# Loading the V projection's weights in two halves of their rows

## The chip, the core and the metric

The kernel runs on one core of a Trainium2 chip. The metric is the device time of one execution in microseconds (us). Each verdict rests on several executions of both kernels on the same chip, and a difference under 2% counts as "same". The profile is of one execution; its span, from first to last instruction, is about 2 us shorter than the device time. The engines are PE (matmuls), DVE (elementwise work and statistics), ACT (activations and copies), POOL, and SP, which here does nothing but issue transfers (DMA).

## The reference, cut to what matters

A transformer block on 2048 tokens of width 512: an adaptive layer norm, attention in which each token looks back at 8 positions two apart, and a gated MLP.

```python
qkv = x @ wqkv                  # wqkv: 512 x 1536, columns of Q, K and V
logits = einsum(q, k at pos - 2*w)          # w = 0..7, 32 heads of 16
o = softmax(logits) @ (v at pos - 2*w);  x = x + ga * (o @ wo)
h = gelu(h2 @ w_gate) * (h2 @ w_up);     x = x + gb * (h @ w_down)
```

## The kernel before

All operations are first collected by a planner, which decides the order on each engine; then they are emitted in that order. The loads from HBM are issued by SP, in this order at the start: rows 0 to 255 of x, the 1 MB of modulation weights (`wm01`), wq in two halves, rows 256 to 511 of x, wk in two halves, wv in one piece, rows 512 to 1023 of x (called **x2** here), and further x and weights.

```python
def load_wqkv(b, p, cuts=1):
    m = DT // cuts
    for i in range(cuts):
        dma(524e3 / cuts, lambda i=i: nc.sync.dma_start(
            out=wqkv[b][:, m * i:m * i + m, :],
            in_=A_wqkv[m * i * P:m * (i + 1) * P, b * D:(b + 1) * D].rearrange("(o p) n -> p o n", p=P)),
            w=[(wqkv[b], k) for k in range(m * i, m * i + m)], pri=p + 0.02 * i)
load_wqkv(0, -998.65, 2)
def load_wk():                       # one operation for the planner, two transfers
    for i in range(2):
        nc.sync.dma_start(out=wqkv[1][:, 2 * i:2 * i + 2, :],
                          in_=A_wqkv[2 * i * P:2 * (i + 1) * P, D:2 * D].rearrange("(o p) n -> p o n", p=P))
dma(524e3, load_wk, w=[(wqkv[1], k) for k in range(DT)], pri=L["wk"])
load_wqkv(2, L["wv"])                # wv, one transfer of 512 KB
load_x(2, 4, L["x1"])
load_x(4, 8, L["x2"])
# ... cut: the other loads ...
# the first 256 tokens: each matmul group is cut by blocks of 128 rows of the weights
cut = ((0,), (1,), (2,), (3,)) if b == 0 else ((0, 1), (2, 3))
for k, dts in enumerate(cut):
    pe(0.23 * len(dts), lambda ...: mm(b, j, ps, range(nj), dts),
       r=[(wqkv[b], dt) for dt in dts] + [(hT[g], dt) for dt in dts], w=[ps], pri=p + 0.01 * k)
```

The tile framework adds the semaphores. It has eight for transfers and hands them out in rotation, in the order of issue; a transfer waits at its issue until the eighth one before it has landed.

## Time and profile before

| | before |
|---|---|
| device time, median of 3 | 242.34 us (242.17 to 242.43) |
| span of the profiled execution | 240.2 us |
| PE busy | 98% of the span |
| PE idle ahead of the first wv matmul | 0.30 us |
| x2 issued by SP, landed | 5.41, 13.66 us |
| PE's steady stretch from | 32.30 us |

The important rows are in the prediction. Four more are from the timelines of the kernel before (start, length, engine, instruction; in brackets the idle time before it and what ended it).

```profile
5.41 2.64 SPq L379 DMA_DIRECT2D x_sg<-in_A_x_dram  x2
...
18.46 0.39 PE L573 MATMUL tp<-ident,xn 128*128 128x128 bf16 x4
...
26.36 0.38 PE L832 MATMUL LT<-Lb,NB 128*128 128x512 bf16 x1 [0.56 <-DVE Lb L827]
...
32.30 1.02 PE L689 MATMUL qkv_ps<-hT,wq 128*128 128x512 bf16 x4 [0.32 <-ACT hT L559]
```

The first row merges SP's issues of the two x loads after wv, of which x2's is the first. The second is four transposes of DVE's `xn`. The third is the first matmul that waits for the maximum of the logits (`Lb`), the end of DVE's long run. The fourth is the last wait of PE before its steady stretch.

### The profile page before, as it was taken

How to read it: one execution, taken by the hardware profiler on the slowest of the kernel's cores; microseconds unless marked ns; L12 is line 12 of the kernel's file. 1: busy time of each engine (PE TensorE's matmuls, PEld its weight loads, DVE VectorE, ACT ScalarE, POOL GpSimd, SP SyncE). 2: the span in 40 equal slices, each digit the busy share in tenths (PEclk: the TensorE clock that was granted, in tenths of full speed). 3: DMA queues.
4: the chain of work that ended last, by engine and by line, in shares of the span. 5: the costliest groups of instructions: out<-in, count | busy, mean ns of one | idle time of the engine just before them, and what ended most of it. 6: DMA issues, size and time to landing. Idle time of an engine off the chain costs nothing.

```text
span 240.2 us, 4193 instructions
## 1 busy us (share of the span) xinstructions
PE 234.3 (98%) x1588; PEld 126.3 (53%) x1588; DVE 160.9 (67%) x307; ACT 159.4 (66%) x298; POOL 12.8 (5%) x35
## 2 busy tenths in 40 slices
PE   7999999999999999999999999999999999999994
PEld 2888545567674557664444444444444444444442
DVE  3699869849997799981899897489455122222222
ACT  4488797699785878669866676846767801666400
POOL 6000210100001000020000002000011000000000
PEclk9999999999999999999999999999999999999999
DMA  6999999999932139512129404100003010000011
GB/s 218 361 367 401 244 305 317 240 257 217 235 60 44 44 87 258 102 36 55 44 60 213 85 3 80 51 22 26 0 1 73 17 44 21 22 0 3 0 44 44
DMA packets 34997, 28.23 MB, mean 118 GB/s; under 512 B 11041, under 2 KB 33314, under 8 KB 34978
## 3 DMA queue, kind: packets, MB, share of 16 engines
q1 hardware_dynamic: 34976, 27.97, 45.8%
q8 instruction: 12, 0.20, 0.4%
q14 instruction: 7, 0.06, 0.1%
q10 hardware_dynamic: 2, 0.00, 0.0%
HBM read 21.40 MB, written 4.21 MB: 107 GB/s over the span
## 4 chain that ended last, share of the span: by engine, by line
PE 86%; DVE 5%; DMA 3%; SPq 2%; ACT 1%; issue 1%; DVEq 0%
PE u_ps L973 20%; PE g_ps L973 20%; PE y_ps L999 20%; PE qkv_ps L689 12%; PE x_ps L932 6%; DMA x_sg<-in_A_x_dram 3%; PE o_ps L907 3%; PE LT L784 3%; DVE st L628 2%; DVE pq L772 1%; ACT hT L559 1%; DVE xn L544 1%; PE ss L867 1%; SPq L423 1%; PE LT L832 1%
## 5 line engine op out<-in xcount | busy, mean ns | idle before, releaser
L973 PE MATMUL g_ps<-h2T,Wg 128*128 128x512 bf16 (+1 forms) x280 | 57.7, 337 | 0.0
L973 PE MATMUL u_ps<-h2T,Wu 128*128 128x512 bf16 (+1 forms) x280 | 57.7, 337 | 0.0
L999 PE MATMUL y_ps<-WdP,hht 128*128 128x512 bf16 (+2 forms) x238 | 50.3, 367 | 0.0
L982 ACT ACTIVATE gl<-g_ps 128x512 bf16<-128x512 f32 x56 | 33.5, 598 | 24.2 <-PE g_ps L973 19.3
L986 DVE TENSOR_TENSOR hht<-gl,ub 128x512 bf16<-128x512 bf16 x56 | 23.4, 422 | 31.0 <-ACT ub L985 30.8
L985 ACT CAST ub<-u_ps 128x512 bf16<-128x512 f32 x56 | 32.8, 585 | 15.3 <-PE u_ps L973 15.1
L973 PEld LDWEIGHTS <-Wg 128*128 128x128 bf16 x280 | 27.1, 98 | 23.3 <-issue 1.7
L973 PEld LDWEIGHTS <-Wu 128*128 128x128 bf16 x280 | 27.1, 98 | 22.2 <-issue 1.3
L772 DVE TENSOR_TENSOR pq<-qT,kT 128x2048 bf16<-128x2048 bf16 x32 | 38.1, 1218 | 0.0
L999 PEld LDWEIGHTS <-hht 128*128 128x128 bf16 x238 | 22.7, 98 | 25.8 <-issue 0.4
L888 DVE TENSOR_TENSOR pv<-e,vR 128x2048 bf16<-128x2048 bf16 x24 | 28.4, 1219 | 0.1
L1007 DVE TENSOR_TENSOR x_sg<-y_ps,x_sg 128x512 bf16<-128x512 f32 (+2 forms) x17 | 10.8, 657 | 26.1 <-PE y_ps L999 26.1
L549 POOL TENSOR_TENSOR rstd<-rstd,neghalf 128x2 f32<-128x2 f32 x12 | 8.8, 731 | 169.2 <-DVE rstd L947 106.7
L689 PE MATMUL qkv_ps<-hT,wq 128*128 128x512 bf16 (+1 forms) x80 | 16.5, 336 | 0.5 <-ACT hT L559 0.5
L689 PE MATMUL qkv_ps<-hT,wk 128*128 128x512 bf16 (+1 forms) x80 | 16.3, 337 | 0.2 <-ACT hT L559 0.2
L689 PE MATMUL qkv_ps<-hT,wv 128*128 128x512 bf16 (+1 forms) x80 | 15.6, 337 | 0.3 <-DMA wv<-in_A_wqkv_dram 0.3
L932 PE MATMUL x_ps<-woP,oT 128*128 128x512 bf16 x64 | 15.3, 379 | 0.0
L939 ACT ACTIVATE xn<-x_sg 128x512 bf16<-128x512 bf16 x16 | 10.0, 627 | 4.2 <-DVE x_sg L936 4.0
L605 ACT ACTIVATE h2T<-h2T,modT,scl 128x512 bf16<-128x512 bf16 (+1 forms) x16 | 11.0, 753 | 2.1 <-DMA h2T<-xn 2.1
L628 DVE BATCH_NORM_STATS2 st<-x_sg 128x6 f32<-128x512 bf16 x16 | 10.2, 681 | 2.8 <-DMA x_sg<-in_A_x_dram 2.8
L689 PEld LDWEIGHTS <-wk 128*128 128x128 bf16 x80 | 8.7, 113 | 5.2 <-issue 0.7
L689 PEld LDWEIGHTS <-wq 128*128 128x128 bf16 x80 | 8.7, 113 | 5.2 <-issue 1.1
(100 smaller groups left out, 217.1 us busy)
## 6 DMA issues: line engine op xcount, KB each, us to landing
vR<-scr SPq DMA_DIRECT2D x24, 260.0 KB, 5.1
vR<-scr SPq DMA_DIRECT2D x8, 264.0 KB, 8.6
out_dram<-x_sg SPq DMA_DIRECT2D x15, 128.0 KB, 1.7
Wu<-in_B_w_up_dram SPq DMA_DIRECT2D x4, 448.0 KB, 8.1
scr<-vT SPq DMA_DIRECT2D x7, 256.0 KB, 7.1
Wg<-in_B_w_gate_dram SPq DMA_DIRECT2D x4, 448.0 KB, 6.5
WdP<-in_B_w_down_dram SPq DMA_DIRECT2D x2, 896.0 KB, 9.8
x_sg<-in_A_x_dram SPq DMA_DIRECT2D x3, 512.0 KB, 8.2
```

Source lines behind the costliest of these rows:

```text
L605: act(act_us(n, 2), lambda dt=dt: nc.scalar.activation(out=dst[:, :, dt, :], in_=dst[:, :, dt, :], func=ACT.Identity, scale=scl[:, off // ...
L628: stats = lambda i=i, st=st, tok=tok: nc.vector.bn_stats(out=st[:, i, :], in_=xrow(tok + P * i))
L689: nc.tensor.matmul(shaped(ps[:, jl, :], g, XB1), lhsT=wqkv[b][:, dt, j + jl:D:4], rhs=columns(hT[g], g, dt, XB1), start=(dt == 0 and (jl = ...
L772: dve(1.145, lambda j=j, wg=wg, no=no, t=pq[m]: nc.vector.tensor_tensor(out=t[:], in0=_ap(q[g][:, j, :], [[0, no], [1, n]]), in1=_ap(kT[:, ...
L888: dve(1.145, lambda jj=jj, jl=jl, wg=wg, t=pv[m]: nc.vector.tensor_tensor(out=t[:], in0=_ap(e[:, wg, :], [[0, 4], [1, n]]), in1=vR[g][jj][ ...
L932: nc.tensor.matmul(x1_ps[:], lhsT=oT[:, j, c4 * P:(c4 + 1) * P], rhs=woP[:, j, :], start=(j == 0), stop=(j == 3))
L973: nc.tensor.matmul(shaped(ps[:, f, :], g, XB2), lhsT=Wt[:, dt, ft * P:(ft + 1) * P], rhs=columns(h2[g], g, dt, XB2), start=(dt == 0), stop ...
L982: act(act_us(SG), lambda gl=gl, ps=gu[0]: nc.scalar.activation(out=gl[:], in_=flat(ps), func=ACT.Gelu_apprx_tanh), r=[gu[0]], w=[gl], pri= ...
L985: act(act_us(SG), lambda ub=ub, ps=gu[1]: nc.scalar.copy(out=ub[:], in_=flat(ps)), r=[gu[1]], w=[ub], pri=p)
L986: dve(0.339, lambda gl=gl, ub=ub, ht=hh[u // 2], u=u: nc.vector.tensor_tensor(out=ht[:, u % 2, :], in0=gl[:], in1=ub[:], op=ALU.mult), r=[ ...
L999: nc.tensor.matmul(y_ps[:], lhsT=hh[u // 2][:, u % 2, f * n + c4 * P:f * n + (c4 + 1) * P], rhs=WdP[:, ft, lo_d:hi_d], start=(ft == 0), st ...
L1007: dve(0.07 + nd * 1.041e-3, lambda y_row=y_row, y_ps=y_ps: nc.vector.tensor_tensor(out=y_row(), in0=y_ps[:], in1=y_row(), op=ALU.add), r=[ ...
```

## The change

Its intent: PE waits for wv at 12 us, so let the first half of wv's rows arrive earlier. The diff, cut to what acts (the rest adds options that are switched off):

```diff
-    load_wqkv(2, L["wv"])
+    def load_wv():
+        for i in range(2):
+            nc.sync.dma_start(out=wqkv[2][:, 2 * i:2 * i + 2, :],
+                              in_=A_wqkv[2 * i * P:2 * (i + 1) * P, 2 * D:].rearrange("(o p) n -> p o n", p=P))
+
+    dma(524e3, load_wv, w=[(wqkv[2], k) for k in range(DT)], pri=L["wv"])
     # ... cut ...
+TREE = ()
+WIDE = 0
```

Instructions and their order are the same on every engine but SP, which has one transfer more.

More of the change, by code (lines that the diff above doesn't have):

```diff
@@ L804, in emit_attention, with most, tree @@
         us = 0.072 + n * 0.52e-3
-        dve(us, lambda: nc.vector.tensor_tensor(out=Lb[:, 0, :], in0=Lb[:, 0, :], in1=Lb[:, 1, :], op=ALU.max),
-            r=[Lb], w=[Lb], pri=p)
+        def most(out, a, b):
+            nc.vector.tensor_tensor(out=out, in0=a, in1=b, op=ALU.max)
+        def tree():
+            most(Lb[:, 0, :], Lb[:, 0, :], Lb[:, 1, :])
+            most(Lb[0:64, 1, :], Lb[0:64, 0, :], Lb[64:128, 0, :])
+            most(Lb[0:32, 0, :], Lb[0:32, 1, :], Lb[32:64, 1, :])
+        joint = g in TREE
+        if joint:
+            dve(3 * us + 0.3, tree, r=[Lb], w=[Lb], pri=p)
+        else:
+            dve(us, lambda: most(Lb[:, 0, :], Lb[:, 0, :], Lb[:, 1, :]), r=[Lb], w=[Lb], pri=p)
         if g in DVEMAX:
@@ L809, in emit_attention @@
             top, all4 = mx
-            def most(out, a, b):
-                nc.vector.tensor_tensor(out=out, in0=a, in1=b, op=ALU.max)
             def spread():
@@ L824, in emit_attention @@
         else:
-            dve(us, lambda: nc.vector.tensor_tensor(out=Lb[0:64, 1, :], in0=Lb[0:64, 0, :], in1=Lb[64:128, 0, :],
-                                                    op=ALU.max), r=[Lb], w=[Lb], pri=p)
-            dve(us, lambda: nc.vector.tensor_tensor(out=Lb[0:32, 0, :], in0=Lb[0:32, 1, :], in1=Lb[32:64, 1, :],
-                                                    op=ALU.max), r=[Lb], w=[Lb], pri=p)
+            if not joint:
+                dve(us, lambda: most(Lb[0:64, 1, :], Lb[0:64, 0, :], Lb[64:128, 0, :]), r=[Lb], w=[Lb], pri=p)
+                dve(us, lambda: most(Lb[0:32, 0, :], Lb[0:32, 1, :], Lb[32:64, 1, :]), r=[Lb], w=[Lb], pri=p)
             def sub_max():
@@ L1018 @@
             mod_keep(mod0, -969)
-            dve(0.34, lambda: nc.vector.tensor_copy(out=wide.t[:, 0, :].rearrange("p (t n) -> p t n", n=P),
+            (gp if WIDE else dve)(0.34, lambda: (nc.gpsimd if WIDE else nc.vector).tensor_copy(out=wide.t[:, 0, :].rearrange("p (t n) -> p t n", n=P),
                                                     in_=_ap(scT[:], [[1, 4], [0, P]])), r=[scT, hT[0]], w=[(wide, 0)],
```

## The prediction

> **What bounds the kernel now.** I read the page first, then the chain of work that ended last in order of time, then the timelines of SP, PE and DVE over the first 30 us, because the change touches only a load that is issued at 4.8 us. From the page (busy time with its share of the span; the shares of the chain by engine; the waits ahead of the group of matmuls that read wv):
>
> ```profile
> span 240.2 us, 4193 instructions
> PE 234.3 (98%) x1588; PEld 126.3 (53%) x1588; DVE 160.9 (67%) x307; ACT 159.4 (66%) x298; POOL 12.8 (5%) x35
> ...
> PE 86%; DVE 5%; DMA 3%; SPq 2%; ACT 1%; issue 1%; DVEq 0%
> ...
> L689 PE MATMUL qkv_ps<-hT,wv 128*128 128x512 bf16 (+1 forms) x80 | 15.6, 337 | 0.3 <-DMA wv<-in_A_wqkv_dram 0.3
> ```
>
> PE is the bound: 86% of the chain, and idle for only 240.2 - 234.3 = 5.9 us of the span. The wait that the change can touch is in the last line: over the whole run PE stood still 0.3 us for wv, once.
>
> Where the other 14% of the chain lies is in the chain in order of time (start, length, what; all us):
>
> ```profile
> 4.83 0.53 SPq L423
> 5.37 0.04 issue
> 5.41 8.25 DMA x_sg<-in_A_x_dram
> 13.66 0.02 issue
> 13.68 2.47 DVE st L628 x4
> ...
> 26.03 0.29 DVE Lb L827
> 26.32 0.04 issue
> 26.36 0.38 PE LT L832
> ...
> 30.23 2.03 ACT hT L559 x3
> 32.26 0.04 issue
> 32.30 7.07 PE qkv_ps L689 x32
> ```
>
> The reader is to see three stretches. SP issues loads one after another; wv (L423) is the last before the 512 KB piece of x, rows 512 to 1023, which I call x2. The landing of x2 at 13.66 starts a run of DVE that lasts to 26.3 us. A short hand-over over PE and ACT follows, and from 32.30 on PE works almost without a gap to the end. So the end moves if x2's landing moves, or the DVE run after it, or the PE work after 32.3. It does not move for PE work done earlier.
>
> Three rows of the timelines (start, length, engine, instruction, and in brackets the idle time before it and what ended it) show the disputed moment:
>
> ```profile
> 12.20 0.63 PE L689 MATMUL qkv_ps<-hT,wv 128*128 128x256 bf16 x4 [0.30 <-DMA wv<-in_A_wqkv_dram]
> ...
> 13.68 2.47 DVE L628 BATCH_NORM_STATS2 st<-x_sg 128x6 f32<-128x512 bf16 x4 [0.27 <-DMA x_sg<-in_A_x_dram]
> ...
> 25.60 0.41 DVE L544 TENSOR_SCALAR xn<-x_sg,mv,rstd 128x512 bf16<-128x512 bf16 x1 [0.51 <-DVE Lb L825]
> ```
>
> PE waits for wv, DVE waits for x2. On DVE's timeline no row between 13.68 and 25.60 has a bracket: in that run DVE never waits for PE or ACT.
>
> **What the Trainium skill says.** (1) "Perfetto Trace Analysis", section DMA Optimizations: splitting DMAs may let some work start sooner, "If DMA engines are generally idle". Here they are not: the page's DMA row is 9 tenths in each slice from 6 to 66 us. A split can bring the first half forward, not the data behind it. (2) "DMA: Bandwidth & Descriptors", section Queues, rings and completion order: each engine consumes descriptors in ring order. The trace agrees: the loads from HBM land in the order of issue, about 0.75 us for each 256 KB (worked out below). (3) The same page, section Why a DMA increments its semaphore by 16 and not by 1: transfers in flight should not share a semaphore. The program has eight of them in rotation, so a transfer waits at issue for the eighth one before it; the trace agrees, with the third x load issued at 6.93, just after the weight load of 1.32 landed at 1.32 + 5.6 = 6.92. (4) "Perfetto Trace Analysis", section DMA Instruction — HWDGE (DVE, Sync): the reported window of such an instruction holds its issue, not the movement of its data. Indeed wv's 512 KB take SP 0.53 us, but PE gets them at 12.20.
>
> **The change part by part.** I compared the order of instructions of both programs. PE, DVE, ACT and POOL have the same instructions in the same order; SP has one more, two loads of wv of 256 KB where there was one of 512 KB. The rest of the diff is switched off (an empty TREE, WIDE = 0). The planner still sees one operation of 524e3 bytes. What moves is this:
>
> (a) First half earlier. Landings before, as issue plus time to landing: the two halves of wk 3.65 + 6.2 = 9.9 and 4.17 + 6.5 = 10.65; x2 5.41 + 8.25 = 13.66. Between wk and x2 lie wv and x2, 1 MB in 3.0 us, so 0.75 us for 256 KB. The whole wv lands at about 10.65 + 1.5 = 12.15, the first half at about 11.4. The new program's first eight wv matmuls need only that half (the wait for the second semaphore stands after them). PE has finished wk at 11.90, so they can start there: the gap of 0.30 us goes. The transposes behind them start at about 12.37 instead of 12.67, because xn is ready at 11.53 + 0.74 = 12.27, and ACT's hT at about 13.0 instead of 13.31. **Gain on PE: 0.30 us; on the path: 0.** DVE is busy or waiting for x2 whatever PE does, and its next result for PE is Lb at 26.03 + 0.29 = 26.32. There PE already waits 0.56 us; it would wait up to 0.86 us instead.
>
> (b) One more transfer in the rotation of eight. Before, x2's issue waited for the transfer eight places ahead, the first piece of x, landed at 0.81 + 3.0 = 3.8, so it did not wait. Now it has the place after, and waits for the 1 MB weight load that lands at 6.92. **x2's issue moves from 5.41 to about 6.95.** In its turn the third x load waits for wq's first half (1.81 + 5.8 = 7.6) and comes at about 7.65 instead of 6.93. The later ones are bounded by landings at 8.4, 9.15, 9.9, 10.65, 11.4 and 12.15, which lie earlier than their old issue times from 10.19 on, so SP has caught up there. Two halves cost SP 0.48 us each (like wq) for one issue of 0.53: 0.4 us, hidden in the same wait.
>
> (c) x2's landing. At 6.95 seven pieces of 256 KB stand ahead of it (wq twice, x, wk twice, wv twice): 7 x 0.75 = 5.2 us, to 12.15. The first load of the program landed 3.0 us after its issue with nothing ahead, of which I estimate 3.0 - 0.75 = 2.25 for everything but the data; x2 could so start to arrive at 9.2. It needs its turn at 12.15 only. **Slack 2.9 us, cost 0.**
>
> (d) Sixteen more tiny completion packets. wk in two pieces and x2 in one run at the same rate, as (a) assumes and the 1.44 us of the next 512 KB (landing at 6.93 + 8.2 = 15.1) bears out: at most 0.05 us on x2's landing.
>
> After wv every transfer waits for the same one as before, as both have moved one place. The sum for the end: 0 (a) + 0 (b, c) + 0 to 0.05 (d).
>
> **Rivals.** *The late issue counts.* If x2 kept its 8.25 us from issue, it would land at 6.95 + 8.25 = 15.2 and the DVE run would begin 1.5 us later: 243.9 us. For it: x2's issue is in the chain. Against it: the 8.25 us are mostly the bytes ahead, by (c), and DMA is 9 tenths busy. Chance about 6%. *The gap on PE counts in full*, if some wait of the stretch to 32 us hangs on PE or ACT after all: 242.34 - 0.3 = 242.0. For it: hT (L559) on ACT is in the chain at 30.23. Against it: that hT comes after Lb and the DVE run. Chance about 15%. *A later shift*: scr<-vT, which SP issues at 16.29 once ACT has written vT, can come 0.3 us earlier and pull the Wu loads behind it. The queue then still holds about 5 us of loads (the 512 KB issued at 10.90 took 9.2 us to land), so nothing lands earlier; worth 0.1 us either way.
>
> **Range and chances.** The sum leaves the time of before: 242.34, and I set 242.3, as the second rival pulls a little lower. The three runs of before span 0.26 us. The second rival gives 0.3 down, (d) and a part of the first rival 0.5 up: 241.8 to 242.9. Two per cent are 4.8 us. A gain of that size would need nearly all of PE's 5.9 us of idle time, a loss three times the first rival: 1% faster, 97.5% same, 1.5% slower.
>
> **What would show it right or wrong.** Right: PE's bracket of 0.30 ahead of wv is gone (a), x2's issue starts at about 6.95 with a time to landing near 6.7 (b), DVE's st still starts at 13.68 within 0.1 (c), PE waits about 0.86 ahead of L832's first matmul, and PE's steady stretch starts at 32.3. Wrong: x2 landing near 15 shows the first rival; Lb ready before 26.2 with x2 landing unchanged shows a dependence of DVE on PE that I do not see; a gap on PE after 40 us would be something that I have not considered.

## The result, and the profile after

The changed kernel took 242.15 us (median of 3; 241.96 to 242.34), before 242.34. The ratio is 0.9993, with a 95% interval of 0.9971 to 1.0016. The change is within the noise.

The page after. (The smaller number of instructions and PE's lower busy time are 18 matmuls missing from the record; the program has as many as before.)

```profile
span 240.0 us, 4177 instructions
...
PE 232.5 (97%) x1570; PEld 125.6 (52%) x1588; DVE 160.9 (67%) x307; ACT 159.1 (66%) x298; POOL 12.8 (5%) x35
...
PE 86%; DVE 5%; DMA 5%; ACT 1%; issue 1%; SPq 0%; DVEq 0%
...
L697 PE MATMUL qkv_ps<-hT,wv 128*128 128x512 bf16 (+1 forms) x79 | 15.5, 337 | 0.1
```

The wait for wv is gone from the last line: no releaser is named any more. In the chain's shares DMA has grown from 3% to 5% and SP's issue has gone from 2% to 0. The chain in order of time shows why:

```profile
1.32 5.33 DMA wm<-in_w_mod_dram
6.65 0.02 issue
6.67 6.77 DMA x_sg<-in_A_x_dram
13.44 0.02 issue
13.46 2.47 DVE st L636 x4
...
26.14 0.38 PE LT L848
...
32.08 2.10 PE qkv_ps L697 x9
```

x2 is issued at 6.67, released by the landing of the modulation weights at 1.32 + 5.33 = 6.65. Before, it was issued at 5.41. Yet it lands at 13.44, so the 1.26 us of later issue are taken off the queue time behind it (6.77 us from issue to landing in place of 8.25). The three PE rows of interest, in the timeline of the changed kernel:

```profile
11.49 0.60 PE L697 MATMUL qkv_ps<-hT,wv 128*128 128x256 bf16 x4
...
17.73 0.59 PE L581 MATMUL tp<-ident,xn 128*128 128x128 bf16 x4
...
26.14 0.38 PE L848 MATMUL LT<-Lb,NB 128*128 128x512 bf16 x1 [0.87 <-DVE Lb L815]
```

wv's first matmul has no bracket, and the wait for `Lb` has grown from 0.56 to 0.87 us. The bracket of 0.30 us was not all that PE had lost to wv, though. From the first wk matmul to the first wv matmul it took 12.20 - 9.99 = 2.21 us before and takes 11.49 - 9.72 = 1.77 us now, 0.44 us less (9.99 and 9.72 are the starts of the wk rows just ahead). Some of it is waited away earlier: the four transposes at 17.73 take 0.59 us in place of 0.39, because inside this merged row they wait 0.20 us for DVE's `xn`. So what PE won at 12 us it waits away at 18 and at 26 us.

This execution runs 0.2 us ahead of the profiled one of before from the start of DVE's run on. That is not the change: the modulation weights, which are issued before anything that changed, landed at 6.65 in place of 6.92. From that landing to x2's landing it is 13.44 - 6.65 = 6.79 us after, and 13.66 - 6.92 = 6.74 before.

### The profile page after: what moved, and what is told of

It reads as the page before. It is cut to its first block, busy times and chain, and to the rows that moved or that the text cites. A ratio compares the mean times of both kernels' runs of the same rounds, so it can differ in the third digit from the quotient of the medians.

```text
span 240.0 us, 4177 instructions
## 1 busy us (share of the span) xinstructions
PE 232.5 (97%) x1570; PEld 125.6 (52%) x1588; DVE 160.9 (67%) x307; ACT 159.1 (66%) x298; POOL 12.8 (5%) x35
## 4 chain that ended last, share of the span: by engine, by line
PE 86%; DVE 5%; DMA 5%; ACT 1%; issue 1%; SPq 0%; DVEq 0%
PE u_ps L989 20%; PE g_ps L989 20%; PE y_ps L1015 20%; PE qkv_ps L697 12%; PE x_ps L948 6%; PE o_ps L923 3%; DMA x_sg<-in_A_x_dram 3%; PE LT L792 3%; DVE st L636 2%; DMA wm<-in_w_mod_dram 2%; DVE pq L780 1%; ACT hT L567 1%; DVE xn L552 1%; PE ss L883 1%; PE LT L848 1%
## 5 line engine op out<-in xcount | busy, mean ns | idle before, releaser
L1015 PE MATMUL y_ps<-WdP,hht 128*128 128x512 bf16 (+2 forms) x230 | 49.8, 366 | 0.4
```

What stands on the lines that cost most here:

```text
L1015: nc.tensor.matmul(y_ps[:], lhsT=hh[u // 2][:, u % 2, f * n + c4 * P:f * n + (c4 + 1) * P], rhs=WdP[:, ft, lo_d:hi_d], start=(ft == 0), st ...
```

## The experiments

The theory: the end hangs on a chain of rigid pieces: x2's landing, then DVE's run and the hand-over to PE's steady stretch, then PE to the end. The change moves x2's issue, not its landing, and moves PE's work where PE has slack. The rivals: the late issue counts; PE's gap counts; something else binds. Eleven kernels were run, all correct.

**The changed kernel again**, with five rounds.

> The changed kernel once more, with more rounds. My theory (the end hangs on when x2 lands, and the split does not move that): a ratio to before of 1.000 within 0.15%, and in the trace x2 landing about 6.8 us after the 1 MB weight load, as in both traces so far (13.66 - 6.92 = 6.74 before, 13.44 - 6.65 = 6.79 after). Rival (the PE gap of 0.30 us counts in full): a ratio of 0.9988 or lower.

Measured: 242.2 us (median of 6) against 242.17, ratio 0.9993 (0.9967 to 1.002). x2 landed 13.54 - 6.75 = 6.79 us after the modulation weights. So no movement is seen, but an interval of 0.5% can't rule out a gain of 0.1% in the times; the traces can, and they show the 0.3 us waited away (0.88 us ahead of `Lb` in this one).

**The extra transfer without the useful half**: wv in halves of its partitions.

```diff
-        for i in range(2):
-            nc.sync.dma_start(out=wqkv[2][:, 2 * i:2 * i + 2, :], in_=<rows 256 i to 256 i + 255>)
+        for lo in (0, 64):
+            nc.sync.dma_start(out=wqkv[2][lo:lo + 64, :, :], in_=<partitions lo to lo + 63>)
```

> wv in two halves of its partitions in place of its rows: the extra transfer in the rotation without a first half that is of use, since every row block needs both. My theory: x2 issued at about 6.7 to 6.9 as in the changed kernel, x2 landing unmoved (6.8 us after the 1 MB weight load), PE's gap of about 0.3 us ahead of wv back, and the gap ahead of L848 0.5 to 0.6 us in place of 0.87; time 242.2 +- 0.3. Rival (the gap counts): 242.5.

Measured: 243.49 us. The expectation failed, because the transfer itself is slower. These are windows of the changed kernel and then of this one (window, length, busy time by engine, granted clock, mean DMA share, GB/s in the last column):

```profile
10.00:11.00 1.00, 1.00 (x12) 1.00 (x10) 0.49 (x3) 0.97 (x4) 0.00 (x0) 1.00 1.10 346
11.00:12.00 1.00, 1.00 (x13) 0.99 (x11) 0.79 (x3) 0.80 (x3) 0.00 (x0) 1.00 1.11 350
```

```profile
10.00:11.00 1.00, 0.97 (x8) 0.71 (x8) 0.69 (x3) 1.00 (x3) 0.00 (x0) 1.00 1.13 213
11.00:12.00 1.00, 0.90 (x8) 0.80 (x8) 0.71 (x2) 0.46 (x3) 0.00 (x0) 1.00 1.13 233
```

While the half-width transfers run, the queue moves 213 to 233 GB/s in place of 346 to 350, at the same DMA share. x2 was issued at 6.87, much as in the changed kernel, and landed 1.0 us late for the bytes ahead of it:

```profile
13.21 0.60 PE L697 MATMUL qkv_ps<-hT,wv 128*128 128x256 bf16 x4 [1.04 <-DMA wv<-in_A_wqkv_dram]
...
14.60 2.47 DVE L636 BATCH_NORM_STATS2 st<-x_sg 128x6 f32<-128x512 bf16 x4 [0.92 <-DMA x_sg<-in_A_x_dram]
...
33.24 1.02 PE L697 MATMUL qkv_ps<-hT,wq 128*128 128x512 bf16 x4 [0.32 <-ACT hT L567]
```

As a test of the rotation it is void. It serves as another: x2 about 1.1 us late gives a steady stretch 1.1 us late.

**More places in the rotation**: wv in four pieces, then in eight (each row block in two halves of its partitions).

```diff
-        for i in range(2): <256 rows each>
+        for dt in range(4): nc.sync.dma_start(out=wqkv[2][:, dt, :], in_=<128 rows>)            # four
+        for k in range(8): nc.sync.dma_start(out=wqkv[2][lo:lo + 64, dt, :], in_=<64 rows>)     # eight
```

> wv in four pieces of one row block: x2 waits for wq's second half and is issued at about 8.2. The queue then still holds data until about 12.0 and a transfer needs some 2.3 us from issue to its first byte. My theory (the queue covers a late issue): x2 lands 6.8 us after the 1 MB weight load as before; time 242.2 +- 0.3. Rival (x2 keeps its 6.8 us from issue to landing): x2 lands at about 15.0, time 243.7.

Measured: 242.08 us. x2 was issued at 8.28, 2.9 us later than in the kernel before, and landed at 13.53, 6.78 us after the modulation weights; the DVE run began at 13.56 and PE's steady stretch at 32.19. This late issue is covered.

> wv in eight pieces (row block by half of the partitions): the eighth piece waits for wk's second half (about 10.5) and x2 waits for the first piece of wv (about 10.8), so x2 is issued at about 11. Now the queue runs dry: first byte of x2 not before about 13.2, landing about 14.7, 1.2 us late. My theory: the DVE run and PE's steady stretch both start 1.0 to 1.5 us late, time 243.2 to 243.7. Rival (x2 keeps 6.8 us from its issue): 17.8, time 246.5. Rival (x2's landing does not set the end): 242.2.

Measured: 244.47 us (median of 4), ratio 1.0098 (1.0059 to 1.0137). The direction is right: x2 is issued at 10.87 and the queue runs dry (95 GB/s from 11 to 12 us, 123 from 12 to 13). But it landed at 16.04, not 14.7. I had not counted that half-width pieces are slow, and there was more, which the next run shows without them.

**Only the rotation**: five loads of 16 rows of 128 bytes ahead of x2.

```diff
     def load_x2():
+        for k in range(5):
+            nc.sync.dma_start(out=spare[0:16, k, :], in_=A_wqkv[0:16, 64 * k:64 * k + 64])
         nc.sync.dma_start(out=xs[1][:], in_=<rows 512 to 1023 of x>)
```

> The changed kernel with five loads of 16 rows of 128 bytes between wv and x2: nearly no bytes, but five more places in the rotation, so x2 waits for wk's second half and is issued at about 10.5, with full-width transfers throughout (the eight pieces and the partition halves also made wv itself slower, which I had not counted). My theory: the queue holds data until about 12.0, x2 needs some 2.3 us plus 1.5 us of data from its issue, so it lands at about 14.2, 0.7 us late, the stretch from DVE's statistics to PE's steady stretch stays 18.6 us, time 242.7 to 243.1. Rival (x2 keeps 6.8 us from its issue): 17.3, time 246. Rival (the late issue is covered here too): 242.2.

Measured: 244.79 us (median of 4), ratio 1.0087 (1.0056 to 1.0118). x2 is issued at 10.61. Windows and rows of its profile:

```profile
11.00:12.00 1.00, 1.00 (x12) 1.00 (x11) 0.73 (x2) 0.78 (x3) 0.00 (x0) 1.00 0.55 84
12.00:13.00 1.00, 1.00 (x16) 0.99 (x14) 0.89 (x1) 0.75 (x3) 0.00 (x0) 1.00 0.79 254
...
20.20:23.60 3.40, 3.31 (x16) 1.84 (x17) 3.40 (x7) 2.24 (x5) 0.00 (x0) 0.50 1.04 358
```

```profile
16.04 1.88 DVE L644 BATCH_NORM_STATS2 st<-x_sg 128x6 f32<-128x512 bf16 x3 [2.70 <-DMA x_sg<-in_A_x_dram]
...
20.29 0.71 PE L589 MATMUL tp<-ident,xn 128*128 128x128 bf16 x4 [2.23 <-DVE xn L560]
...
35.17 1.02 PE L705 MATMUL qkv_ps<-hT,wq 128*128 128x512 bf16 x4 [0.32 <-ACT hT L575]
```

The queue is dry at 11 to 12 us (84 GB/s): here is the edge beyond which a late issue counts, as the theory has it. The size was wrong by two things. The trace records the completion of a transfer in sixteen parts. Of x2's, fifteen came by 14.54, close to the 14.2 expected, and one at 16.02. In the same stretch a 16 KB packet of the instruction queue runs from 11.67 for 1.99 us. That this packet held back the last part is likely. The eleven other traces without an early disturbance have one such packet too, of 1.0 to 1.1 us, later in the run. There the last part of a load is at most 0.4 us behind the other fifteen ahead of the packet, and 0.8 to 1.5 us behind them on the first or second load that lands after it. But the record doesn't name what carried a part, and in the two disturbed traces at the end of this section a part trails by 1.4 to 1.9 us with no such packet before it, so the cause stays inferred. And PE, left idle for 2.23 us, has a granted clock of 0.50 from 20.2 to 23.6 us; the run from DVE's statistics to the steady stretch takes 19.1 us in place of 18.6. The eight pieces show the same: 2.56 us of idle PE ahead of 20.30, then a clock of 0.50 from 19.8 to 23.2.

Both profiles caught the worse of two cases. Of the four executions with five small loads, the one with a granted clock of 0.998 took 243.69 us, the three at 0.991 to 0.993 took 244.69 to 245.12. Of the four of the eight pieces, the two at 0.998 and 0.999 took 243.9 and 244.23 us, the two at 0.993 took 244.72 and 246.14. With 242.17 us for the kernel before on the eight pieces' chip, their late x2 costs 1.7 us or more also where the clock holds; for the five small loads one such execution is too little to say.

The runs together, from the same rows of each profile; the last five are described below. "Run" is steady stretch minus statistics, "rest" is span minus steady stretch:

| kernel | x2 issued | DVE statistics | PE steady from | run | rest |
|---|---|---|---|---|---|
| before | 5.41 | 13.68 | 32.30 | 18.62 | 207.9 |
| changed | 6.67 | 13.46 | 32.08 | 18.62 | 207.9 |
| changed, again | 6.76 | 13.56 | 32.19 | 18.63 | 208.1 |
| four pieces | 8.28 | 13.56 | 32.19 | 18.63 | 207.8 |
| partition halves | 6.87 | 14.60 | 33.24 | 18.64 | 208.2 |
| five small loads | 10.61 | 16.04 | 35.17 | 19.13 | 207.6 |
| eight pieces | 10.87 | 16.06 | 34.97 | 18.91 | 207.7 |
| three fillers on PE | 6.70 | 13.49 | 32.13 | 18.64 | 207.9 |
| twelve fillers on PE | 6.75 | 13.55 | 33.68 | 20.13 | 207.9 |
| x2 ahead of wv | 4.97 | 13.39 | 32.54 | 19.15 | 208.7 |
| wv and x2 woven | 5.37, 7.46 | 13.12 | 31.74 | 18.62 | 208.6 |
| reads of vR earlier | 6.59 | 13.38 | 32.01 | 18.63 | 207.9 |

In the first seven rows the run and the rest are rigid, to within 0.1 us and 0.3 us, as long as the clock holds. There x2's landing is what sets the end, and it doesn't follow its issue until the queue is dry. The run is longer where PE was made late by more than its slack (twelve fillers, x2 ahead of wv), and the rest where PE waits for `pv` (x2 ahead of wv, woven).

**PE's slack**: three and twelve more matmuls of 128x512 ahead of the first wv matmul of the changed kernel.

```diff
             def mm(b, j, ps, jls, dts):
+                if g == 0 and b == 2 and j == 0 and dts == (0, 1):
+                    filler(ps.t, 3)          # 12 in the second kernel
```

> The changed kernel with three more matmuls of 128x512 (0.65 us) on PE just ahead of the first wv matmul: PE is made later than in the kernel before, with all loads as changed. My theory (PE has slack up to Lb): the gap ahead of L850 or so (the matmul that waits for Lb) shrinks from 0.87 to about 0.2 us, PE's steady stretch starts where it did, time 242.2 +- 0.3. Rival (PE's time here counts): 242.8.

Measured: 242.07 us, with the steady stretch from 32.13. The wait for `Lb` shrank to 0.44 us:

```profile
18.40 0.39 PE L581 MATMUL tp<-ident,xn 128*128 128x128 bf16 x4
...
26.19 0.38 PE L850 MATMUL LT<-Lb,NB 128*128 128x512 bf16 x1 [0.44 <-DVE Lb L817]
```

It lost 0.43 us for 0.65 us of matmuls; I had expected it to fall to 0.2. The first wv matmul came the whole 0.65 us later (12.17 in place of 11.49, in an execution 0.03 us behind). The other 0.2 us came out of the wait for `xn`: the four transposes take 0.39 us again.

> The same with twelve matmuls (2.6 us). My theory: the slack of 0.87 us on PE is used up and the rest, 2.6 - 0.9 = 1.7 us, reaches the end: 243.9 (243.5 to 244.3). Rival (the slack is much larger, other engines wait only for DMA): 242.2. Rival (everything counts): 244.8.

Measured: 243.59 us (median of 4), ratio 1.0067 (1.0053 to 1.0081). The steady stretch began at 33.68 with x2 landing unmoved (statistics at 13.55), so 1.5 us of the 2.6 came through and 1.1 us was slack. Here DVE does wait inside its run:

```profile
18.63 1.38 DVE L552 TENSOR_SCALAR xn<-x_sg,mv,rstd 128x512 bf16<-128x512 bf16 x4 [1.22 <-ACT rstd L562]
```

ACT computes this `rstd` after `hT`, for which it waited 2.84 us for PE's transposes; and the matmul ahead of which PE waited for `Lb` has no bracket any more. So PE's lateness reaches the end by way of ACT, not through the wait for `Lb` alone. Both sides of the theory's claim are shown: PE may be later by 0.65 us at no cost, and is not free without bound.

**x2 ahead of wv**, with wv's halves behind it.

```diff
-    wv rows 0-255; wv rows 256-511; x2
+    x2; wv rows 0-255; wv rows 256-511
```

> The changed kernel with x2 issued ahead of wv's halves: x2 lands 1.5 us earlier, wv 1.5 us later. My theory: DVE loses its gap of 0.27 us ahead of its statistics, but PE waits for wv about 1.2 us more, uses up its slack of 0.87 us ahead of the matmul that waits for Lb, and gives back what DVE won: time 242.0 to 242.5. Rival (only DVE counts): 241.9. Rival (PE's wait counts): 243.4.

Measured: 243.25 us, above what I expected and nearer to the last rival. In its timeline of PE:

```profile
13.03 0.63 PE L709 MATMUL qkv_ps<-hT,wv 128*128 128x256 bf16 x4 [1.07 <-DMA wv<-in_A_wqkv_dram]
...
32.54 1.02 PE L709 MATMUL qkv_ps<-hT,wq 128*128 128x512 bf16 x4 [0.31 <-ACT hT L579]
...
40.92 0.40 PE L935 MATMUL o_ps<-pv,F 128*32 128x256 bf16 x8 [0.54 <-DVE pv L922]
```

PE's wait for wv (1.07 us) was larger than its slack allowed, DVE waited 0.26 us for ACT's `rstd` at 17.50, and the steady stretch began 0.4 us late. A wait appeared that shows in neither kernel: 0.54 us for `pv`, DVE's product with the V tiles `vR`, which are written to memory and read back. `vR` itself landed 1.2 us later than in the changed kernel (36.12 in place of 34.95). That second chain is close behind the first.

**wv and x2 woven**, both in halves.

```diff
-    wv rows 0-255; wv rows 256-511; x2
+    wv rows 0-255; x2 rows 512-767; wv rows 256-511; x2 rows 768-1023
```

> The changed kernel with x2 in two halves too, woven with wv's: wv rows 0 to 255, x2 rows 512 to 767, wv rows 256 to 511, x2 rows 768 to 1023. wv's second half lands 0.75 us later than now, x2's first half 0.75 us earlier than x2 now. My theory: DVE's gap of 0.29 us ahead of the statistics goes and PE has no new wait (its second half of wv is needed 0.9 us after the transposes start), so the end comes 0.25 us earlier: 241.9 to 242.0, ratio to before 0.998 to 0.999. Rival (the DVE run hangs on something else): unchanged, ratio 0.9993 to 1.000.

Measured: 242.3 us (median of 5), ratio 1.0012 (0.9999 to 1.0026). The rows of its timelines of DVE and PE:

```profile
13.12 2.46 DVE L648 BATCH_NORM_STATS2 st<-x_sg 128x6 f32<-128x512 bf16 x4
...
31.74 1.02 PE L709 MATMUL qkv_ps<-hT,wq 128*128 128x512 bf16 x4 [0.31 <-ACT hT L579]
...
35.40 4.63 DVE L922 TENSOR_TENSOR pv<-e,vR 128x2048 bf16<-128x2048 bf16 x4 [1.82 <-DMA vR<-scr]
...
40.08 0.40 PE L935 MATMUL o_ps<-pv,F 128*32 128x256 bf16 x8 [0.50 <-DVE pv L922]
```

DVE's gap is gone and the steady stretch begins 0.34 us earlier than in the changed kernel, as expected. Then PE waits 0.50 us for `pv`, and `pv` waits for the reads of `vR`, which land at 35.28, as in the kernel before. The gain is given back there: my theory was right for the first 32 us and wrong for the end. The two chains are in fact nearly level in the kernel before: its merged row of 32 `o_ps` matmuls lasts 1.20 us, against 1.06 where `vR` lands by 34.6, so I take PE to wait about 0.14 us for `pv` there already.

**The reads of vR earlier**: the last quarter of w_up's load issued behind the four reads of `vR`, alone and with the woven order.

```diff
-    Wu rows 0-127; 128-255; 256-383; 384-511; woP; vR x4
+    Wu rows 0-127; 128-255; 256-383; woP; vR x4; Wu rows 384-511
```

> The changed kernel with the last quarter of Wu issued behind the four vR reads in place of ahead of them, a control for the next run: vR is read about 1 us earlier. My theory: in the changed kernel PE's o_ps matmuls do not wait for pv, so an earlier vR is worth nothing: 242.15, ratio to before 0.998 to 1.000.

Measured: 241.9 us (median of 4; 241.75 to 242.03), ratio 0.9976 (0.995 to 1.0001). `vR` landed 0.9 us earlier than in the changed kernel (34.07 in place of 34.95), and DVE's statistics (13.38) and the steady stretch (32.01) are again 18.63 us apart, with a rest of 207.9 us as in the changed kernel, so the trace shows no gain. The interval holds 1, and three of the twelve runs of before on that chip had a granted clock of 0.993 or less, so whether this change alone gains is open.

> The woven order of wv and x2 together with the early vR reads. The woven run started PE's steady stretch at 31.74 in place of 32.1 to 32.2, and then waited 0.50 us at 40.08 for pv, which hangs on the vR reads (landed 35.27). My theory: with vR 1 us earlier this wait goes, and the end comes 0.3 to 0.4 us earlier than in the changed kernel: ratio to before 0.997 to 0.9985, about 241.7. Rival (the gain is lost at another wait after 40 us): ratio 0.999 to 1.001.

Measured: 241.9 us (median of 7), ratio 0.9969 (0.9943 to 0.9995). The profiled execution was disturbed, so the kernel was run once more:

> The woven order with the early vR reads once more, because the profiled execution of the first run was disturbed (its 1 MB weight load landed 1.8 us late[...], and PE's clock was halved for 3.4 us). My theory: in an undisturbed execution PE's steady stretch starts at 31.6 to 31.8 and runs without the wait of 0.50 us at 40 us, the span is 207.9 us longer than that start, 239.5 to 239.7, and the ratio to before is 0.9975 to 0.999. Rival (the wait at 40 us stays or another takes its place): span 240.0 or more, ratio 0.999 to 1.001.

Measured: 241.92 us (median of 7) against 242.53, ratio 0.9971 (0.9946 to 0.9997). The profile again caught a disturbed execution (244.68 us): one of sixteen parts of the first large load landed 1.4 us behind the others, at 8.25, and PE's clock was 0.50 from 10.4 to 13.8. In that trace the steady stretch runs without the wait for `pv`, but this shows nothing: it began at 34.80, 3 us later than in the woven run, with `vR` landed at 35.35. Of the fourteen executions of the two submissions, ten have a granted clock of at least 0.999 and took 241.62 to 242.00 us; the ten such executions of before took 241.78 to 243.37. The spans of this kernel's ten are 239.6 to 240.1 us, where I had expected 239.5 to 239.7: two lie in that range, three fit the rival (240.0 or more), five lie between, and no profile shows where the rest went. So this is the fastest version seen, by about 0.3% in the ratio and well within 2%, and its lead over the early reads alone (241.9) is not shown.

## Why the prediction was right

The forecast of 242.3 us and "same" held, and so did the mechanism of each step; one size in step (a) did not. The times alone would decide little: the interval of the ratio, 0.9971 to 1.0016, is wider than the 0.12% of the second rival. The traces decide.

- Step (a), the gap of 0.30 us goes and is waited away ahead of `Lb`: the wait grew to 0.87 us (0.86 forecast), and three filler matmuls put PE later again without cost. That the number fits so well is luck. PE gained 0.44 us at wv (0.47 in the second trace), not 0.30: the prediction let it start at 11.90, where the last wk row ends, but rows of matmuls overlap by about 0.17 us in these timelines. And it lost 0.16 to 0.20 us of this ahead of the transposes at 18 us, in a wait that the prediction didn't have. The claim that DVE is busy or waiting for x2 whatever PE does holds up to about 1.1 us of lateness. Beyond that DVE waits for ACT, and ACT for PE; twelve fillers and x2 first show it.
- Step (b), x2's issue moves to the landing of the modulation weights: 6.67 after 6.65 (about 6.95 forecast, in a run whose weights landed 0.27 us earlier). For the same reason DVE's statistics start at 13.46, a little outside the forecast of 13.68 within 0.1. The sentence that after wv every transfer waits for the same one as before holds only from the eighth transfer behind wv on; for the seven ahead of it, x2 first, (b) itself says otherwise.
- Step (c), the queue covers the late issue: shown by four pieces, where an issue at 8.28 made no difference. The edge lies between there and 10.6, where the five small loads left the queue dry. The slack of 2.9 us was an estimate; the runs bracket it between 1.6 us (8.28 - 6.67) and 3.9 us (10.61 - 6.67) but don't measure it. An estimate from the five small loads agrees: fifteen of x2's parts came 14.54 - 10.61 = 3.93 us after an issue into the dry queue, so an issue up to 13.44 - 3.93 = 9.5 would do, 2.8 us after 6.67.
- Step (d), the completion packets of one more transfer: not visible, the landings differ by 6.74 to 6.79 us from the weights in all three traces.
- The rivals: a late issue that counts from issue to landing was refuted by four pieces. The gap on PE counting in full was refuted by the 0.87 us ahead of `Lb` and by the three fillers. The shift of `scr<-vT` did occur, in part: its issue came at 15.55 in place of 16.29 and it landed at about the same time, 23.58 in place of 23.63.
- The quotation on splitting runs two sentences together: "Perfetto Trace Analysis", section DMA Optimizations, says without a condition that splitting may let some transfers start sooner, and makes idle DMA engines the condition for the whole task to complete sooner. The runs agree with both: wv's first matmul came sooner, the end did not.

What the prediction did not have is the second chain over `vR`. It did no harm here, but it is the reason why a true gain at x2 (the woven order) did not reach the end.

## What to carry to other kernels

A wait that shows on the bounding engine is worth its length only if the engine has no later wait that absorbs it: find the next wait on the same engine before the stretch that runs to the end, and ask whether what ends it would come earlier too. Splitting a transfer brings its first half forward, but also takes a place among the transfers in flight and delays the issue of what follows. While the queue was full that was free here (x2 issued at up to 8.28). When it ran dry (issue at 10.61 and 10.87) it cost more than the bytes, since PE sat idle for over 2 us and then ran at a clock of 0.50 for 3.4 us. When a chain is shortened by a few tenths of a us, look first how far behind the next one lies.

## What the Trainium skill lacked or had wrong

- "TensorE: Matmul & The Clock Gate", section What's actually happening, gives half clock after at least one idle window of about 3.4 us. The length agrees (a clock of 0.50 for 3.4 us in three runs), but a fully idle window is not needed: gaps of 2.23 and 2.56 us, in a window in which PE was busy over a third of the time, were enough (1.25 of 3.43 us busy from 16.8 to 20.23 in the run with five small loads).
- "Runtime: NRT & Kernel Launch", section Instruction fetch mechanics, calls the cost of crossing a 16 KB block of instructions mostly hidden. In the run with five small loads a 16 KB packet of 1.99 us ran while x2 was in flight, and one of sixteen parts of x2's completion came 1.5 us behind the other fifteen. That the fetch caused it is inferred.
- No page that I read says what a rotation of eight completion semaphores does to the issue of later transfers: one more transfer ahead moved x2's issue from 5.41 to 6.67 us.
